# Cosformer attention and a GELU feed-forward on one core: attention recast token-major in full-array matmuls of 65 columns, x transposed by DMA, every load cast to bf16 on Pool's queue

## The chip, the cores and the metric

The kernel runs on one NeuronCore of a Trainium2 chip. A core has a matmul engine (PE, TensorE) with its weight loads (PEld), a vector engine (DVE), a scalar engine (ACT), a general engine (POOL, GpSimd), a sequencer that mostly issues DMAs (SP), and 16 DMA engines. POOL, SP and ACT can each issue DMAs on a queue of their own. Matmul results land in PSUM, eight banks of 512 f32 per partition; everything else is in SBUF. The metric is device time in microseconds (us) of one execution; the median of several runs is compared.

## What is computed

Eight batches of eight heads, 576 tokens, head dimension 64. Each head has linear attention with a cosine and a sine copy of relu(q) and relu(k). The result, as 4608 tokens of 512, goes through two dense layers of 512x2048 and 2048x512 with a sigmoid GELU between them.

```python
B, H, S, D = q.shape                      # 8, 8, 576, 64
theta = np.pi / 2.0 * np.arange(S) / S
cos_w, sin_w = np.cos(theta)[None, None, :, None], np.sin(theta)[None, None, :, None]
def phi(x, c, s):
    r = np.maximum(x, 0.0)
    return np.concatenate([r * c, r * s], axis=-1)
q_p, k_p = phi(q, cos_w, sin_w), phi(k, cos_w, sin_w)
kv  = np.einsum('bhsf,bhsd->bhfd', k_p, v)
z   = np.sum(k_p, axis=2)
num = np.einsum('bhsf,bhfd->bhsd', q_p, kv)
den = np.einsum('bhsf,bhf->bhs', q_p, z)[..., None] + 1e-06
x   = (num / den).transpose(0, 2, 1, 3).reshape(B * S, H * D)
h   = x @ w_in
out = (h / (1.0 + np.exp(-1.702 * h))) @ w_out
```

## The kernel before, in words

**Feed-forward.** The 4608 tokens are cut into nine blocks of 512. `xT` holds x transposed, 512 features in four groups of 128 partitions, all tokens along the row. In block `i`, `mm1(i, fc)` makes one of 16 slices of h: four matmuls of 512 columns (L373) into a PSUM tile `mm`, then a GELU on ACT into bf16 `g` (L378). `mm2` makes the output of 128 tokens at a time: 16 matmuls of 512 columns (L409), a copy to `ysb` on ACT (L419), and a store from POOL's queue (L421). The loop over `n` from 0 to 31 (L542) writes out a block's order by hand: `n` below 16 are the `mm1`, the others groups of four `mm2` matmuls. Block 0 goes through its four output tiles side by side, so that each quarter of `w_out` is needed in turn.

**Attention of the next batch.** Between those groups of block `i`, for `i` from 0 to 6, stand pieces of the attention of batch `b = i + 1`, put at chosen `n` by `at(n, ...)` (L511 to L541). Batch 0 is done ahead of block 0 (L444 to L504). Every engine runs its instructions in the order written. A batch has 576 tokens and a block 512, so the feed-forward falls behind attention by 64 tokens a block, and blocks 7 and 8 have no attention beside them.

**Steps of a batch.** A chunk `c` is 128 tokens (the last, the tail, 64). Tokens of the first 512 are dealt four to a partition, so that a partition's load is 1 KB in a row.

- Loads (`load_part`, `load_tail`, L76 to L103): q, v and k in f32, on SP's queue, each a main part and a tail. Batch 0's tails go on ACT's queue.
- `prep_q` (L216): relu of q to bf16 `qn`, no weights yet.
- Transpose of q: on PE for batches 0 and 1 (`transpose_pe`, L231), by five DMA transposes on SP's queue for the rest (`transpose_dma`, L243). After it DVE multiplies by cosine and sine of each token (`trig`, L241 and L253), giving `qT`, head pairs on partitions, tokens along the row.
- `prep_v` (L262): v times cosine and v times sine, two copies, into `vt`, with two more columns of cosine and sine for the denominator. `prep_k` (L255): relu of k into `kr`.
- `unit_kv` (L277): 40 matmuls of 130 columns, two heads side by side in halves of the array (L285).
- `unit_den` (L306): 32 matmuls of 144 columns in quarters of the array give denominators with tokens along the row (L315); DVE inverts them and splits each number into two bf16 parts.
- `unit_spread` (L359), for each half of the tokens: eight matmuls (L333) repeat the inverses over the 64 rows of each head; ACT copies them to SBUF (L352).
- `unit_num` (L364), for each half: 16 matmuls of 288 columns in quarters of the array (L346), then DVE multiplies by the inverses, straight into `xT` (L357). No transpose of x is needed.

PSUM is split into four `mm` and four `at` tiles of one bank each.

**Order of the loads.** Batch 0's loads stand at the head of SP's queue. The weights are cast from f32 to bf16 by DMAs on POOL's queue. Small instructions that touch a loaded tile keep them in order: POOL's copy of one element of v (L463) holds back `w_in`, a DMA of two bytes of `w_in` on SP (L466) holds back batch 1's loads, POOL's copy from batch 1's k (L479) holds back `w_out`, and one more DMA on SP (L481) holds back batch 2's loads. From batch 3 on, `load_all` runs at `n` = 1 of a block, behind the DMA transposes on SP's queue.

`warmup(n)` (L69) issues matmuls on zeros before and between the steps of batch 0.

Of the kernel before, what the change touches and what calls it, by code (L numbers as in the profile page):

```python
# [2 lines left out]

# [16 lines left out]
GE = mybir.AluOpType.is_ge  # L20
LE = mybir.AluOpType.is_le
ADD = mybir.AluOpType.add
SUB = mybir.AluOpType.subtract
AND = mybir.AluOpType.bitwise_and
# [4 lines left out]
def kernel(  # L29
# [13 lines left out]
    NP = H // 2  # L43
    FC = d_ff // 128
    TB = 512
    NBLK = B * S // TB
    HF = S // 2
    NSEG = 4
    SEG = S // NSEG
    VW = 2 * D + 2  # L50
# [3 lines left out]
    two = ctx.enter_context(tc.tile_pool(name="two", bufs=2))  # L54
    ps = ctx.enter_context(tc.tile_pool(name="ps", bufs=1, space=PSUM))
    ctx.enter_context(tc.manual_schedule())

# [6 lines left out]
    def at_tile():  # L66
        return ps.tile([128, TB], F32, name="at", bufs=4)
# [5 lines left out]

    state = {b: {} for b in range(B)}

    def load_part(t, src, b, h0, h1):  # L76
        nc.sync.dma_start(  # L77
            out=t[:, 256 * h0:256 * h1].rearrange("p (h e) -> p h e", h=h1 - h0),
            in_=src[b, h0:h1, 0:512, :].rearrange("h (p c) d -> p h (c d)", c=4))

    def load_tail(t, src, b, on):
        on.dma_start(
            out=t[0:64, 2048:2560].rearrange("p (h d) -> p h d", h=H),
            in_=src[b, :, 512:576, :].rearrange("h p d -> p h d"))

    SRC = (("qf", q), ("vf", v), ("kf", k))

    def load_new(b):
        for name, _ in SRC:
            state[b][name] = two.tile([128, 2560], F32, name=name)  # L90

    def load_tails(b, on):
        for name, src in SRC:
            load_tail(state[b][name], src, b, on)

    def load_mains(b):
        for name, src in SRC:
            load_part(state[b][name], src, b, 0, H)

    def load_all(b):  # L100
        load_new(b)
        load_mains(b)
        load_tails(b, nc.sync)  # L103

    load_new(0)
    s0 = state[0]
    load_part(s0["qf"], q, 0, 0, 8)
    load_part(s0["vf"], v, 0, 0, 8)
    load_part(s0["kf"], k, 0, 0, 4)
    load_part(s0["kf"], k, 0, 4, 8)  # L110
    load_tails(0, nc.scalar)


    tmp = ExitStack()
    tpool = tmp.enter_context(tc.tile_pool(name="tmp", bufs=1))
# [3 lines left out]
    pos_i = const.tile([128, 5], I32)  # L119
    nc.gpsimd.iota(pos_i[:, 0:4], pattern=[[1, 4]], base=0, channel_multiplier=4)  # L120
    nc.gpsimd.iota(pos_i[:, 4:5], pattern=[[1, 1]], base=512, channel_multiplier=1)
    sel_i = tpool.tile([128, NSEG, 2], I32)
    for j in range(NP):

        nc.gpsimd.iota(sel_i[32 * j:32 * j + 32], pattern=[[-4, NSEG], [16 if j % 2 else -16, 2]],
                       base=-16 * (j % 2), channel_multiplier=1)
    col_i = tpool.tile([128, S], I32)
    nc.gpsimd.iota(col_i[:, 0:512], pattern=[[1, 4], [4, 128]], base=0, channel_multiplier=0)
    nc.gpsimd.iota(col_i[:, 512:576], pattern=[[1, 64]], base=512, channel_multiplier=0)
    id_i = tpool.tile([128, 128], I32)  # L130
    nc.gpsimd.iota(id_i, pattern=[[1, 128]], base=0, channel_multiplier=-1)
    row_i = const.tile([128, 1], I32)
    nc.gpsimd.iota(row_i, pattern=[[0, 1]], base=0, channel_multiplier=1)
    pos_f = const.tile([128, 5], F32)
    nc.vector.tensor_copy(pos_f, pos_i)
    col_f = tpool.tile([128, S], F32)
    nc.vector.tensor_copy(col_f, col_i)
    ident = const.tile([128, 128], BF16)
    nc.vector.tensor_scalar(ident, id_i, 0.0, None, op0=EQ)
    sinw = const.tile([128, 5], F32)  # L140
    cosw = const.tile([128, 5], F32)
    nc.scalar.activation(sinw, pos_f, AF.Sin, scale=scale)
    nc.scalar.activation(cosw, pos_f, AF.Sin, scale=-scale, bias=halfpi)
    trig = const.tile([128, 2, S], BF16)
    nc.scalar.activation(trig[:, 0, :], col_f, AF.Sin, scale=-scale, bias=halfpi)
    nc.scalar.activation(trig[:, 1, :], col_f, AF.Sin, scale=scale)
# [3 lines left out]
    sel_f = tpool.tile([128, NSEG, 2], F32)  # L150
    sel_a = tpool.tile([128, NSEG, 2], F32)
    sel = const.tile([128, NSEG, 2, 64], BF16)
    nc.vector.tensor_scalar(sel_f, sel_i, 2.0, None, op0=LE)
    nc.vector.scalar_tensor_tensor(sel_a, sel_i, 0.0, sel_f, op0=GE, op1=MUL)
    nc.vector.tensor_copy(sel, sel_a.unsqueeze(3).to_broadcast([128, NSEG, 2, 64]))
    tmp.close()

    gpool = ctx.enter_context(tc.tile_pool(name="gpool", bufs=18))
    ypool = ctx.enter_context(tc.tile_pool(name="ypool", bufs=4))

    kr = one.tile([128, 5, NP, 128], BF16, name="kr")
    vt = one.tile([128, 5, H, VW], BF16, name="vt")
    nc.gpsimd.memset(kr[64:128, 4], 0.0)
    nc.gpsimd.memset(vt[64:128, 4], 0.0)
    for c in range(5):
        np_ = 128 if c < 4 else 64
        for cs, w in enumerate((cosw, sinw)):
            nc.gpsimd.tensor_copy(
                vt[:np_, c, :, 128 + cs:129 + cs],
                w[:np_, c:c + 1].unsqueeze(1).to_broadcast([np_, H, 1]))  # L170

    e0 = float(np.float32(1e-6).astype(ml_dtypes.bfloat16))
    e1 = float(np.float32(1e-6 - e0).astype(ml_dtypes.bfloat16))
    e2 = float(np.float32(1e-6 - e0 - e1).astype(ml_dtypes.bfloat16))
    ones = const.tile([3, 128], BF16)
    epsm = const.tile([3, SEG], BF16)
    by_row = const.tile([128, 8], F32)
    bits = const.tile([128, 2], I32)  # L180
    nc.gpsimd.memset(ones, 1.0)
    nc.vector.tensor_scalar(row_i, row_i, 3, None, op0=AND)
    for n, (r, x) in enumerate(((0, -65535.0), (1, -255.0), (1, -65536.0), (2, -256.0), (0, e0), (1, e1), (2, e2))):
        nc.gpsimd.tensor_scalar(by_row[:, n:n + 1], row_i, float(r), x, op0=EQ, op1=MUL)
    nc.gpsimd.tensor_scalar(by_row[:, 0:1], by_row[:, 0:1], by_row[:, 1:2], -1.0, op0=ADD, op1=ADD)
    nc.gpsimd.tensor_tensor(by_row[:, 1:2], by_row[:, 2:3], by_row[:, 3:4], op=ADD)
    nc.gpsimd.tensor_copy(bits, by_row[:, 0:2])
    nc.gpsimd.tensor_tensor(by_row[:, 7:8], by_row[:, 4:5], by_row[:, 5:6], op=ADD)
    nc.gpsimd.tensor_tensor(by_row[:, 7:8], by_row[:, 7:8], by_row[:, 6:7], op=ADD)
    nc.gpsimd.tensor_copy(epsm, by_row[0:3, 7:8].to_broadcast([3, SEG]))  # L190

    zbuf = [one.tile([128, NP, 2, 48], BF16, name=f"zbuf{i}") for i in range(2)]
    for t in zbuf:
        nc.gpsimd.memset(t, 0.0)

    w_in_sb = one.tile([128, NP, d_ff], BF16)
    w_out_sb = one.tile([128, FC, d_model], BF16)
    win_r = moe_w_in.rearrange("(kc p) f -> p kc f", p=128)  # L200
    wout_r = moe_w_out.rearrange("(fc p) d -> p fc d", p=128)
    xT = one.tile([128, NP, B * S], BF16)


    def prep_new(b):
        s = state[b]
# [9 lines left out]
    def prep_q(b, par, on=nc.vector):  # L216
# [11 lines left out]
        if par == 0:  # L228
            relu(on, o[0:64, 4], it)
# [360 lines left out]
```

## Time and profile before

| | us |
|---|---|
| median of 5 runs | 315.0 (314.68 to 316.48) |
| the profiled execution: time | 316.48 |
| its span | 314.7 |
| ACT busy | 136.1 |
| L373 and L409, 512-column matmuls, busy | 128.3 and 125.7 |
| out stores, POOL's issues (L421), busy | 29.5 |

The span is what the profile covers; the run's time lies a little over it. PE's busy time counts a matmul from its start to its end, and ends overlap the next start, so that 512-column matmuls have a mean of 380 ns while they start 216 ns apart. PEld is the loading of weights, which overlaps matmuls. DMA share is the mean busy share of the 16 DMA engines; packets under way together can bring it over 1. Rows such as `L285 PE MATMUL at<-vt,kr 128*64 128x130` read: line 285, result tile from moving and weight tile, the part of the array in use (rows x columns), partitions x columns of the moving tile. In brackets at the end of a timeline's row stands how long the engine had been idle and what ended it.

### The profile page before, as it was taken

The page shows a single profiled execution, that of the slowest core. Times are in us where ns is not written, and L with a number is a line of the kernel's source. Part 1 is how long each engine was busy: PE and PEld are TensorE (multiplying, and loading weights), DVE is VectorE, ACT ScalarE, POOL GpSimd, SP SyncE. Part 2 cuts the span into 40 slices and gives each one's busy share as a digit, 9 for nine tenths or more (in the row PEclk, how much of TensorE's full clock was granted, in tenths as well). Part 3 has the DMA queues.
Part 4 walks back from the last instruction along what each step waited for, and adds up shares of the span by engine and source line. Part 5 has one row for each costly group of instructions (what it writes and reads, how often), then busy time and mean ns, then how long its engine had stood idle before and what let it go on. Part 6 is the DMA issues. An engine that isn't in the chain of part 4 may idle for free.

```text
span 314.7 us, 5588 instructions
## 1 busy us (share of the span) xinstructions
PE 298.8 (95%) x2170; PEld 140.6 (45%) x2208; DVE 134.8 (43%) x341; ACT 136.1 (43%) x263; POOL 47.3 (15%) x106
## 2 busy tenths in 40 slices
PE   8779959999999999999999999999999999999994
PEld 3443434445444544454445444544454444444443
DVE  4860782296339523952295229531953110000000
ACT  5545411355335533553355434543463346226511
POOL 7800060100121011000210120001200220011021
PEclk9998979999999999999999999999999999999998
DMA  7999979996945692489157924791510320011022
GB/s 218 274 203 261 206 116 200 340 240 163 319 98 115 187 284 80 112 245 244 45 116 222 260 65 118 226 251 70 108 36 0 69 67 0 35 67 34 2 67 67
DMA packets 60126, 45.85 MB, mean 146 GB/s; under 512 B 28932, under 2 KB 57860, under 8 KB 60100
## 3 DMA queue, kind: packets, MB, share of 16 engines
q1 hardware_dynamic: 51028, 31.60, 39.2%
q0 software_dynamic: 7328, 13.37, 19.0%
q10 hardware_dynamic: 1744, 0.52, 0.8%
q8 instruction: 17, 0.28, 0.4%
q14 instruction: 9, 0.07, 0.1%
HBM read 36.70 MB, written 9.44 MB: 147 GB/s over the span
## 4 chain that ended last, share of the span: by engine, by line
PE 83%; issue 8%; DMA 5%; POOL 1%; ACT 0%; DVE 0%; SPq 0%; DVEq 0%; ACTq 0%; POOLq 0%
PE mm L409 39%; PE mm L373 35%; DMA vf<-in_v_dram 3%; PE at L346 3%; PE at L285 2%; DMA w_out_sb<-in_moe_w_out_dram 2%; PE at L315 1%; POOL w_in_sb L465 1%; PE mm L433 1%; PE at L333 1%; ACT g L378 0%; DVE xT L357 0%; SPq L77 0%; DVE ysb L438 0%; POOL junk L479 0%
## 5 line engine op out<-in xcount | busy, mean ns | idle before, releaser
L373 PE MATMUL mm<-xT,w_in_sb 128*128 128x512 bf16 x559 | 128.3, 382 | 2.0 <-DVE xT L357 1.2
L409 PE MATMUL mm<-w_out_sb,g 128*128 128x512 bf16 x539 | 125.7, 380 | 1.4 <-DMA w_out_sb<-in_moe_w_out_dram 0.3
L378 ACT ACTIVATE g<-mm 128x512 bf16<-128x512 f32 x144 | 85.5, 598 | 55.6 <-PE mm L373 53.3
L373 PEld LDWEIGHTS <-w_in_sb 128*128 128x128 bf16 x576 | 55.9, 98 | 68.9 <-issue 3.9
L409 PEld LDWEIGHTS <-g 128*128 128x128 bf16 x560 | 52.0, 98 | 63.9 <-issue 3.2
L421 POOL DMA_DIRECT2D out_dram<-ysb x54 | 29.5, 549 | 234.7 <-ACT invb L352 126.1
L419 ACT COPY ysb<-mm 128x512 f32<-128x512 f32 x34 | 19.9, 590 | 87.4 <-PE mm L409 57.6
L357 DVE TENSOR_TENSOR xT<-at,invb 128x288 bf16<-128x288 f32 x60 | 23.3, 450 | 65.2 <-PE at L346 65.2
L352 ACT COPY invb<-at 128x288 f32<-128x288 f32 x60 | 19.7, 421 | 20.4 <-PE at L333 20.4
L438 DVE COPY ysb<-mm 128x256 f32<-128x256 f32 x1 | 0.4, 424 | 56.7 <-PE mm L433 56.7
L253 DVE TENSOR_TENSOR qT<-qTr,trig 128x1152 bf16<-128x1152 bf16 x24 | 16.6, 753 | 17.4 <-DMA qTr<-qn 14.4
L274 DVE TENSOR_SCALAR vt<-vf,cosw 128x512 bf16<-128x512 f32 (+1 forms) x40 | 18.9, 481 | 2.1 <-DMA vf<-in_v_dram 2.1
L214 DVE TENSOR_SCALAR qn<-qf 128x512 bf16<-128x512 f32 (+2 forms) x52 | 14.4, 340 | 9.8 <-DMA qf<-in_q_dram 9.8
L274 DVE TENSOR_SCALAR vt<-vf,sinw 128x512 bf16<-128x512 f32 (+1 forms) x36 | 17.2, 479 | 0.0
L285 PE MATMUL at<-vt,kr 128*64 128x130 bf16 x320 | 11.7, 233 | 4.7 <-DVE kr L214 2.9
L285 PEld LDWEIGHTS <-kr 128*64 128x64 bf16 x320 | 10.2, 116 | 8.2 <-DVE kr L214 3.4
L214 DVE TENSOR_SCALAR kr<-kf 128x1024 bf16<-128x1024 f32 (+1 forms) x23 | 12.7, 601 | 0.0
L72 PE MATMUL mm<-warm 128*128 128x512 bf16 x39 | 11.1, 446 | 1.2 <-DVE halfpi L118 1.2
L346 PE MATMUL at<-qT,kvs 64*64 64x288 bf16 x240 | 10.6, 289 | 0.2 <-DVE den L321 0.2
L346 PEld LDWEIGHTS <-kvs 64*64 64x64 bf16 x256 | 6.2, 106 | 6.7 <-issue 6.4
L323 DVE TENSOR_SCALAR den<-at 128x144 f32<-128x144 f32 x7 | 2.2, 307 | 13.4 <-PE at L315 13.3
L324 DVE RECIPROCAL den<-den 128x144 f32<-128x144 f32 x7 | 7.4, 1053 | 0.2
(72 smaller groups left out, 97.2 us busy)
## 6 DMA issues: line engine op xcount, KB each, us to landing
qf<-in_q_dram SPq DMA_DIRECT2D x8, 1024.0 KB, 5.9
vf<-in_v_dram SPq DMA_DIRECT2D x8, 1024.0 KB, 9.3
kf<-in_k_dram SPq DMA_DIRECT2D x6, 1024.0 KB, 12.3
out_dram<-ysb POOLq DMA_DIRECT2D x38, 128.0 KB, 2.5
out_dram<-ysb POOLq DMA_DIRECT2D x16, 256.0 KB, 2.6
kf<-in_k_dram SPq DMA_DIRECT2D x4, 512.0 KB, 9.8
w_in_sb<-in_moe_w_in_dram POOLq DMA_DIRECT2D x4, 512.0 KB, 9.1
w_out_sb<-in_moe_w_out_dram POOLq DMA_DIRECT2D x4, 512.0 KB, 9.3
```

Of the source, the lines that this page charges most:

```text
L214: on.tensor_scalar(o, i, 0.0, None, op0=MAX)
L253: nc.vector.tensor_tensor(s["qT"][:, j], s["qTr"][:, j].unsqueeze(1).to_broadcast([128, 2, S]), trig, op=MUL)
L274: on.tensor_scalar(o, i, w, None, op0=MUL)
L285: nc.tensor.matmul(kv4[j // 2][w:w + 64, j % 2], kr[:, c, j, 64 * hh:64 * hh + 64], vt[:, c, 2 * j + hh, :], start=(c == 0), stop=(c == 4))
L346: nc.tensor.matmul(tiles[j][w:w + 64, 0:HF], s["kvs"][j][r:r + 64, cs, :], s["qT"][r:r + 64, j, cs, ds(hf * HF, HF)], start=(cs == 0), sto ...
L352: nc.scalar.copy(t, tiles[j][:, 0:HF])
L357: nc.vector.tensor_tensor(xT[:, j, ds(b * S + hf * HF, HF)], tiles[j][:, 0:HF], state[b]["sb", j, hf], op=MUL)
L373: nc.tensor.matmul(hps, w_in_sb[:, kc, ds(fc * 128, 128)], xT[:, kc, ds(i * TB, TB)], start=(kc == 0), stop=(kc == NP - 1))
L378: nc.scalar.activation(g, hps, AF.Gelu_apprx_sigmoid)
L409: nc.tensor.matmul(yps, gT[fc][:, ds(t * 128, 128)], w_out_sb[:, fc, :], start=(fc == 0), stop=(fc == FC - 1))
L419: nc.scalar.copy(ysb, cur[t])
L421: nc.gpsimd.dma_start(out=out[row:row + (n - 1) * step + 1:step, :], in_=ysb[p0:p0 + n, :])
```

## The change

Attention is written anew; the feed-forward, its 512-column matmuls and its stores stay.

- The cosine and sine weights move from q's transposed form and from v to q and k in token-major form. `prep` takes the relu and the weight in one DVE operation: two operations per chunk for q (into `qn`, 128 features a head) and two for k (into `kp`). v is only copied (`prep_v`), with one column of ones beside each head's 64.
- `unit_kv` is 40 matmuls with full 128x128 weights (`kp` of a chunk and head) and 65 columns (v and the ones). The last chunk's lower rows are zeros. Two copies on DVE bring the result to `kvs`.
- `unit_num` works on one chunk: eight matmuls, one a head, with `qT` of the chunk as 128x128 weights and the 65 columns of `kvs`. Tokens are on partitions, so numerator and denominator of a token and head lie in one row; DVE adds 1e-6, inverts eight numbers a token and multiplies 512 columns by them, into `xb`. `unit_den`, `unit_spread` and their tables are gone.
- q's weighted form is transposed by DMA on SP's queue (`turn_q`, five a batch, 1024 columns each), x as well (`turn_x`, five a batch, 512 columns each). Only the first four chunks of batch 0 are transposed on PE, both q and x, with copies by ACT.
- The tail chunk of batch 0 is left for block 0: its `prep` and `turn_q` at `n` = 4, its `unit_num` and `turn_x` at `n` = 9.
- All loads go on POOL's queue and are cast to bf16 on the way, but for batch 0's tails of k and v (f32, SP's queue). Nothing holds them back but buffers and that each POOL DMA waits, in the built program, for the landing of the eighth POOL DMA before it. Order: q, k, v of batch 0, four `w_in`, q of batch 1 and its tail, q's tail of batch 0, one `w_out`, k and v of batch 1 with tails, three `w_out`, all of batch 2. From batch 3 on `load_all` stands at `n` = 1 of the block two before.
- `at` tiles are two of two banks each. The start has 18 and 14 warm-up matmuls; before it had 21, 14 and 4.

```diff
-    HF = S // 2
-    NSEG = 4
-    SEG = S // NSEG
-    VW = 2 * D + 2
+    NC = 5
+    VW = 66
...
     def at_tile():
-        return ps.tile([128, TB], F32, name="at", bufs=4)
+        return ps.tile([128, 2, 512], F32, name="at", bufs=2)
...
+    def load_main(b, n):
+        state[b][n] = t = two.tile([128, 2048], BF16, name=n)
+        nc.gpsimd.dma_start(out=t.rearrange("p (h e) -> p h e", h=H),
+                            in_=SRC[n][b, :, 0:512, :].rearrange("h (p c) d -> p h (c d)", c=4))
+
+    def load_tail(b, n, on=None, dt=BF16):
+        state[b][n, 4] = t = two.tile([64, 512], dt, name=n + "t" + str(dt == F32))
+        (on or nc.gpsimd).dma_start(out=t.rearrange("p (h d) -> p h d", h=H),
+                                    in_=SRC[n][b, :, 512:576, :].rearrange("h p d -> p h d"))
...
+    load_tail(0, "k", nc.sync, F32)
+    load_tail(0, "v", nc.sync, F32)
+    load_main(0, "q")
+    nc.gpsimd.iota(pos_i[:, 0:4], pattern=[[1, 4]], base=0, channel_multiplier=4)
+    nc.gpsimd.iota(pos_i[:, 4:5], pattern=[[1, 1]], base=512, channel_multiplier=1)
+    load_main(0, "k")
+    nc.gpsimd.iota(id_i, pattern=[[1, 128]], base=0, channel_multiplier=-1)
+    load_main(0, "v")
+    for g in range(4):
+        load_w_in(g)
+    load_main(1, "q")
+    load_tail(1, "q")
+    load_tail(0, "q")
+    load_w_out(0)
+    for n in "kv":
+        load_main(1, n)
+        load_tail(1, n)
+    for g in range(1, 4):
+        load_w_out(g)
+    load_all(2)
...
+    def prep(b, n, c):
+        o = state[b]["qn"] if n == "q" else kp
+        for cs, w in enumerate((cosw, sinw)):
+            nc.vector.tensor_scalar(o[:rows(c), c, :, cs * D:cs * D + D], part(b, n, c), 0.0, w[:rows(c), c:c + 1],
+                                    op0=MAX, op1=MUL)
+
+    def prep_v(b, c):
+        nc.vector.tensor_copy(vt[:rows(c), c, :, 0:D], part(b, "v", c))
...
+    def turn_q(b, c):
+        nc.sync.dma_start_transpose(out=q_slot(b, c)[:, :, 0:rows(c)],
+                                    in_=state[b]["qn"][:rows(c), c].rearrange("p h e -> p (h e)"))
+
+    def turn_x(b, c):
+        nc.sync.dma_start_transpose(out=xT[:, :, ds(b * S + c * 128, rows(c))],
+                                    in_=state[b]["xb"][:rows(c), c].rearrange("p h d -> p (h d)"))
...
+    def unit_kv(b):
+        kv = at_tile()
+        for h in range(H):
+            o = kv[:, h // 4, ds(h % 4 * (D + 1), D + 1)]
+            for c in range(NC):
+                nc.tensor.matmul(o, kp[:, c, h, :], vt[:, c, h, 0:D + 1], start=(c == 0), stop=(c == NC - 1))
+        kvs = two.tile([128, 2, 4, VW], BF16, name="kvs")
...
+    def unit_num(b, c):
+        nm = at_tile()
+        for h in range(H):
+            nc.tensor.matmul(nm[:, h // 4, ds(h % 4 * (D + 1), D + 1)], q_slot(b, c)[:, h, :],
+                             state[b]["kvs"][:, h // 4, h % 4, 0:D + 1], start=True, stop=True)
...
+        nc.vector.tensor_scalar(den[:r], nm4[:, :, :, D], 1e-6, None, op0=ADD)
+        nc.vector.reciprocal(inv[:r], den[:r])
+        nc.vector.tensor_tensor(state[b]["xb"][:r, c].rearrange("p (n h) d -> p n h d", n=2), nm4[:, :, :, 0:D],
+                                inv[:r].unsqueeze(3).to_broadcast([r, 2, 4, D]), op=MUL)
...
+    warmup(18)
+    for c2 in range(2):
+        tp = at_tile().bitcast(BF16)
+        for c in (2 * c2, 2 * c2 + 1):
+            prep(0, "q", c)
+            for h in range(H):
+                nc.tensor.transpose(tp[:, c % 2, ts(h, 128)], s0["qn"][:, c, h, :], ident)
+            nc.scalar.copy(qT[:, :, ts(c, 128)], tp[:, c % 2].rearrange("p (h t) -> p h t", h=H))
+    for c in (4, 0, 1, 2, 3):
+        prep(0, "k", c)
+    for c in (4, 0, 1, 2, 3):
+        prep_v(0, c)
+    warmup(14)
+    unit_kv(0)
...
+    unit_num(0, 0)
+    unit_num(0, 1)
+    turn_x_pe(0)
+    unit_num(0, 2)
+    turn_x_pe(1)
+    unit_num(0, 3)
+    turn_x_pe(2)
     first = [mm_tile() for _ in range(4)]
+    mm1_part(first[0], 0, 0, 0, 256)
+    turn_x_pe(3)
+    for fc in (1, 2):
+        mm1_part(first[fc], 0, fc, 0, 256)
+    for fc in range(3):
+        mm1_part(first[fc], 0, fc, 256, 512)
+        gelu(first[fc], fc)
+    mm1_part(first[3], 0, 3)
+    gelu(first[3], 3)
...
+        if i == 0:
+            at(4, prep, 0, "q", 4)
+            at(4, turn_q, 0, 4)
+            at(9, unit_num, 0, 4)
+            at(9, turn_x, 0, 4)
+        elif i + 2 < B:
+            at(1, load_all, i + 2)
         if b < B:
+            k0, k1, k2 = (5, 17, 19) if i == 0 else (0, 12, 17)
             at(k0, prep_new, b)
+            for c in range(NC):
+                at(k0 + c // 2, prep, b, "q", c)
+                at(k0 + c // 2, turn_q, b, c)
+                at(k0 + 5 + c // 2, prep, b, "k", c)
+                at(k0 + 9 + c // 3, prep_v, b, c)
             at(k1, unit_kv, b)
+            for c in range(NC):
+                at(k2 + 2 * c, unit_num, b, c)
+                at(k2 + 2 * c, turn_x, b, c)
```

## Prediction

> **What bounds the kernel now.** I read the page first: which engine is full, and when its clock falls.
>
> ```profile
> PE 298.8 (95%) x2170; PEld 140.6 (45%) x2208; DVE 134.8 (43%) x341; ACT 136.1 (43%) x263; POOL 47.3 (15%) x106
> ...
> PEclk9998979999999999999999999999999999999998
> ```
>
> PE is busy for 95% of the span, and no other engine for half. So what counts is PE's own time in each block, and the stretches early on where PE has nothing to do or a lower clock. Busy time by stretch, cut where PE begins a block's first matmul (PE alone; columns: PE busy, granted clock, DMA share, GB/s), gives the prices:
>
> ```profile
> 15.00:22.00 7.00, 5.52 (x126) 1.00 1.22 203
> 63.34:95.61 32.27, 32.01 (x243) 1.00 0.80 200
> 95.61:127.45 31.84, 31.58 (x245) 1.00 0.66 164
> ...
> 223.11:254.94 31.83, 31.57 (x244) 1.00 0.25 53
> 254.94:282.57 27.63, 27.52 (x128) 1.00 0.10 39
> ```
>
> A block that carries a batch's attention takes 31.84 us, one without it 27.63, which is 128 matmuls of 512 columns, 216 ns from start to start. Attention therefore costs 4.21 us of PE per batch. Blocks 1 to 6, which do batches 2 to 7, run from 63.34 to 254.94, 191.6 us. The start ends at 21.98, and block 0 takes 41.4 us up to 63.34. By 27.63 + 4.21 it would take 31.8, so 9.5 us lie there. The timelines of both, in order of time, show what ends the waits:
>
> ```profile
> 6.89 0.99 DVE L214 TENSOR_SCALAR qn<-qf 128x512 bf16<-128x512 f32 x3 [2.05 <-DMA qf<-in_q_dram]
> ...
> 15.07 1.32 PE L285 MATMUL at<-vt,kr 128*64 128x130 bf16 x40 [1.62 <-ACT kr L212]
> ...
> 21.98 0.81 PE L373 MATMUL mm<-xT,w_in_sb 128*128 128x512 bf16 x3 [0.57 <-DVE xT L357]
> ```
>
> ```profile
> 39.68 0.39 POOL L479 COPY junk<-kf 1x1 f32<-1x1 f32 x1 [24.05 <-DMA kf<-in_k_dram]
> 40.02 4.54 POOL L480 DMA_DIRECT2D w_out_sb<-in_moe_w_out_dram  x4
> ...
> 43.19 2.47 PE L285 MATMUL at<-vt,kr 128*64 128x130 bf16 x40 [2.89 <-DVE kr L214]
> ```
>
> The start is a chain: loads, preparation, 40 matmuls at 15.07, 6.9 us of attention, first matmul. In block 0 PE waits 2.89 us for batch 1's k and goes on at half clock (40 matmuls in 2.47 us instead of 1.32). POOL's touch of `kf` holds the `w_out` loads back until 40.02.
>
> **The change, part by part.** *Attention on PE, blocks 1 to 6.* The 120 matmuls a batch of L285, L315, L333 and L346, which share the array between tiles, go; 40 for `kv` and 40 for the numerators come, each with 128x128 weights and 65 columns. No row has this shape. The price of a matmul with full weights follows from the narrowest views (PE, then PEld):
>
> ```profile
> 34.89 0.22 PE L237 MATMUL at<-ident,qn 128*128 128x128 bf16 x1
> ...
> 34.89 0.39 PE L237 MATMUL at<-ident,qn 128*128 128x128 bf16 x4
> ```
>
> ```profile
> 108.18 0.11 PEld L373 LDWEIGHTS <-w_in_sb 128*128 128x128 bf16 x2
> ```
>
> Three further 128-column matmuls add 0.39 - 0.22 us, 56 ns each, weight loads included. 512 columns take 216 ns. A line through both gives 0.416 ns a column plus 2.7 ns, so 30 ns for 65. Two weight loads of 98 ns fit in 0.11 us, so one can follow another in some 15 ns, which would hide behind 30. The upper end is 56 ns, as if a short stream waited for its weights. I take 32, near the line, and 0.1 us a batch for entries into the sections: 80 x 0.032 + 0.1 = 2.66 us instead of 4.21 (bounds 2.5 and 4.6). Six blocks: 6 x 1.55 = 9.3, and 0.4 that block 1 lost over the others: **9.7 us** (bounds 10.7 and -1.9).
>
> The Trainium skill speaks against this ("TensorE: Matmul & The Clock Gate", sections "LDWEIGHTS" and "Weight-path perf modes"): weights load at 1.2 columns per ns, 107 ns for 128, and the fast mode was measured at about twice that, some 53 ns. By that, an estimate, 80 loads would take 4.3 us a batch and the gain would be nothing. The row with two loads in 0.11 us speaks for the shorter one.
>
> *DVE and ACT.* Per batch DVE loses the four multiplications by `trig`, ten scalings of v, five relus of k, the spread's arithmetic and four products of each half. It gains 20 `prep` operations, five copies and five times (add, reciprocal, product). Their price: 0.48 us by the f32 rows of L274 at 512 elements, 0.33 by the bf16 row of L241 (750 ns for 1152). I take 0.33; the product is priced as the 128x512 copy from PSUM, 0.68 (L417), with 0.17 for each small operation: 1.0 us a chunk. 25 x 0.33 + 5 x 1.0 = 13 us of 30: hidden, at 0.48 too. ACT loses the eight copies of L352.
>
> *Transposes.* Before, five transposes by DMA a batch turn 512 columns of q a token. Now five turn 1024 columns of q and five more 512 of x: three times the work, and PE's transposes of q in block 0 become DMA's too.
>
> ```profile
> qTr<-qn SPq DMA_TRANSPOSE x30, 3.0
> ...
> w_in_sb<-in_moe_w_in_dram POOLq DMA_DIRECT2D x4, 512.0 KB, 9.1
> ```
>
> SP spends 1.27 us on each (median of L248). Twice that for the wide ones: 5 x 2.5 + 5 x 1.27 = 19 us of SP a block, and the last q turn is used 24 us into it. x has 10 us to spare in blocks 1 to 6. Cover exists as long as SP keeps below 30 us a block; beyond that PE waits for SP one to one. SP no longer issues loads, so turns pass none on its own queue, but share the DMA engines with POOL's. In block 0 chunk 3 of x is issued about 5.4 us before block 1 needs it and takes 1.0 + 1.3 + 3.0: 0.5 us of wait.
>
> *Loads.* All on POOL, cast on the way, each waiting for the landing of the eighth before it alone. `w_in` wrote 512 KB in 2.6 us at 203 GB/s. A main part of q, k or v also reads 1 MB and writes 512 KB, but in pieces half as long: 2.6 us if bytes count, 5.2 if pieces do. The plain loads of before moved 341 GB/s between 58.0 and 63.3, 3.1 us for 1 MB, and I take that, nearer to what these loads are. Before, three such and three tails landed from 2.0 to 13.9, so a tail costs 11.9 - 9.3 over 3 = 0.87. Now two tails, three mains and 0.4 for POOL's later start: 2.0 + 1.7 + 9.3 + 0.4 = 13.4 for v, 10.3 for k, 7.2 for q. DVE ends q at 9.8, k at 13.1 (two operations on its tail from 9.8, eight from 10.5), v's four copies at 14.7, and PE starts at 15.0. 40 matmuls: 16.3; `kvs` 16.9; first numerator 17.3; four chunks at 1.0: 18.3 to 21.3; PE turn and ACT copy 1.0: 22.3. Of the first 16 matmuls 1.3 us (twelve of 256 columns on the first two chunks) is done by then: they end at 22.3 + 3.45 - 1.3 = 24.5, where before they end at 21.98 + 0.4 + 3.45 = 25.9. Both lose 1.7 us more to the half clock there. **1.4 us** (bounds: with 0.48 on DVE 0; with 5.2 a main part -4).
>
> In later blocks the six loads stand ahead of the outputs on POOL (L421). An issue of 512 pieces takes 1.0 us (L465) and one of 128 some 0.55 (L421), so 1024 cost about 1.6: 3 x 1.6 + 3 x 1.0 = 8 us from n=1 on, and the first output comes at n=19, 16 us in. Hidden; were it not, `ysb`'s four buffers would hold ACT's copies and then PE's `mm` tiles.
>
> *Block 0.* At 26.2 PE starts n=4, at 31.4 it is past n=9 and wants the turn of q's last 64 tokens of batch 0. That tail stands ninth to tenth in the queue: `w_in` to 23.8, q of batch 1 to 26.9, two tails to 28.7; two `prep` 0.7; the turn 3.0 and 1.3 more for its width: 33.7. **A new wait of 2.3 us** with everything of PE behind it. Then 0.3 and eight groups of 0.86: 40.9 at `unit_kv`. `w_out`'s first part and batch 1's k and v are 3.4 MB, 4.6 with the turns of q beside them: at 3.1 a MB and 0.7 for the last copies ready between 40.0 and 43.7; I take 42.5, 1.6 us of wait (bounds 0 and 2.8). 1.3 for `kv`, 1.7 half clock as before, 14 groups 12.1, five numerators 1.3, 0.5 for x: block 1 starts at **59.4** instead of 63.34.
>
> Sum: 3.9 up to block 1, start included, and 9.7 after it: 13.6 us. The profiled execution has a span of 314.7 and a time of 316.48; the median of five is 315.0, and I take the gain from that: **301 us**.
>
> POOL's issues meet DVE work too. The Trainium skill ("SBUF — State Buffer", "SBUF: two separate sides", the box on the SWDGE trap) says that DVE's fast modes keep POOL from writing descriptors, one long issue instead of a short one. Here L465 took 1.0 us an issue beside DVE work, so I add nothing.
>
> **Rivals.** *Weights show* (56 ns): blocks 1 to 6 gain -1.9 to 0, the start stays: 315 - 3.9 + 1.9 = 313. For it: no row has short streams behind full loads. Against: the two loads in 0.11.
> *DMA becomes the bound* (slower). Share times length gives work per block: 0.66 x 31.8 = 21 with loads, 0.25 x 31.8 = 8.0 without, 0.10 x 27.6 = 2.8 for outputs. So loads 13, turns 5.2. Three times the turns: 13 + 15.6 + 2.8 = 31.4 for a block of 30.3. It decides once turns or loads are late for the next block, above 31.9 of real time. At a tenth more, 34.5: 6 x 2.6 - 3.9 = 12 slower, 327. For it: turns and loads were never under way together before. Against: shares reach 1.22 (15 to 22), so share overstates work.
> *Casting goes by pieces* (5.2 us): three mains 6.3 later, of which DVE's spare time takes 1: start 5 later, block 0 some 3: 309.
> *Block 0 without its waits and half clock*: 2.3 + 1.6 + 1.7 less: 295.4.
>
> **Numbers.** Forecast 0.50, weights 0.12, DMA 0.18, pieces 0.10, no waits 0.10. About 0.5% (1.6 us) is what a measurement can tell from no change. Faster: 0.50 + 0.20 + half of 0.12 = 0.76; same 0.06; slower 0.18. Range 294 to 313: it leaves out DMA and a little at both ends; the forecast's own is 296 to 306.
>
> **What would show it.** Right: blocks 1 to 6 of 30.2 us, starts of the 65-column matmuls 30 to 35 ns apart, a PE wait before the numerator of batch 0's last chunk, DVE under 45%. Wrong: 50 ns and more there; PE waiting on turns in blocks 1 to 6; the first 512-column work after 25; a DMA share near 1.2 throughout.

## The result, and the profile after

The changed kernel takes 316.92 us (median of 38 runs, 315.96 to 319.61) where the kernel before takes 315.69 (75 runs beside them). The ratio is 1.0046, 95% interval 1.0032 to 1.0059: slower by about half a per cent, where 301 us was forecast. The medians here and below are of all runs, while the ratios leave out the few slow ones, among them one of 1070.35 us of the kernel with six turns of q on PE and two buffers. The profiled execution (319.01 us) has a span of 317.2 us, the one of before (316.48 us) 314.7: the spans differ by 2.5 us where the medians differ by 1.2.

The page, its span, busy times and the clock that was granted to TensorE in 40 slices:

```profile
span 317.2 us, 4917 instructions
...
PE 289.3 (91%) x1867; PEld 144.7 (46%) x1900; DVE 103.6 (33%) x347; ACT 115.9 (37%) x193; POOL 97.3 (31%) x115
...
PEclk9897999669997999999999999999999999999999
```

PE is 9.5 us less busy than before (298.8), yet the span grew: PE's share fell from 95% to 91%, and the clock shows a new hole in slices 8 and 9 (56 to 71 us). Cut by blocks (columns: PE busy and instructions, granted clock, DMA share, GB/s), the loss has a place:

```profile
24.98:73.44 48.46, 35.29 (x230) 0.87 1.14 155
73.44:107.33 33.89, 31.73 (x205) 0.95 1.23 156
107.33:137.43 30.10, 29.89 (x205) 1.00 1.13 154
227.73:257.83 30.10, 29.89 (x205) 1.00 0.47 94
257.83:285.46 27.63, 27.53 (x127) 1.00 0.11 39
```

Block 0 took 41.36 us before and takes 48.46; block 1 took 32.27 and takes 33.89; the later blocks with a batch took 31.6 to 32.3 and take 30.1. The start is 3.0 us later (24.98 against 21.98). So up to block 1's first matmul 10.1 us are lost (73.44 against 63.34), blocks 1 to 6 give 7.2 back (184.4 against 191.6), the end 0.4: 2.5 us, the difference of the spans.

What PE waits for in block 0 is in the timeline of the changed kernel (start, length, engine, line, operation; in brackets the idle time before it and what ended it):

```profile
28.19 0.54 DVE L163 TENSOR_SCALAR qn<-qtFalse,cosw 64x512 bf16<-64x512 bf16 x1 [2.63 <-DMA qtFalse<-in_q_dram]
29.02 1.30 SPq L174 DMA_TRANSPOSE qT_tail<-qn  x1
36.13 0.43 PE L200 MATMUL at<-kvs,qT_tail 128*128 128x65 bf16 x8 [0.87 <-DMA qT_tail<-qn]
36.21 0.35 DVE L163 TENSOR_SCALAR qn<-q,cosw 128x512 bf16<-128x512 bf16 x1 [7.22 <-DMA qT_tail<-qn]
36.93 16.80 SPq L174 DMA_TRANSPOSE qT<-qn  x5
53.82 18.68 SPq L178 DMA_TRANSPOSE xT<-xb  x6
62.48 0.69 DVE L208 TENSOR_TENSOR xb<-at,inv 128x512 bf16<-128x512 f32 x1 [13.76 <-DMA xT<-xb]
63.32 0.59 PE L200 MATMUL at<-kvs,qT 128*128 128x65 bf16 x8 [9.33 <-DVE den L206]
```

Read it downwards as one chain. The turn of q's tail is issued at 29.02 and lands 7.1 us later. `qn` has one buffer, so DVE cannot write batch 1's q before that: 7.22 us idle. SP then needs 16.8 us to issue five turns of q. Behind them, at 53.82, stands the turn of x for batch 0's tail, though its product was ready at 40.4. `xb` has one buffer as well, so DVE's product for batch 1's first chunk waits 13.76 us for that turn, and PE, which needs the `at` buffers emptied, waits 9.33. The clock is halved for 10.24 us (58.21 to 68.45). About half of that passes while PE still waits; PE works through the other 5.1 us at half speed, some 2.6 us of loss.

### The profile page after: what moved, and what is told of

Same layout as the page of the kernel before. It is cut to its first block, busy times and chain, and to the rows that moved or that the text cites. A ratio compares the mean times of both kernels' runs of the same rounds, so it can differ in the third digit from the quotient of the medians.

```text
span 317.2 us, 4917 instructions
## 1 busy us (share of the span) xinstructions
PE 289.3 (91%) x1867; PEld 144.7 (46%) x1900; DVE 103.6 (33%) x347; ACT 115.9 (37%) x193; POOL 97.3 (31%) x115
## 4 chain that ended last, share of the span: by engine, by line
PE 74%; DMA 17%; SPq 4%; ACT 1%; issue 1%; DVE 1%; POOL 0%; ACTq 0%; POOLq 0%; DVEq 0%
PE mm L251 34%; PE mm L216 34%; DMA qtFalse<-in_q_dram 5%; DMA qT<-qn 4%; SPq L174 4%; PE at L200 3%; DMA k<-in_k_dram 3%; DMA xT<-xb 3%; DMA qT_tail<-qn 2%; PE at L187 2%; ACT g L221 1%; PE mm L275 1%; POOL q L76 0%; DVE qn L163 0%; DVE xb L208 0%
## 5 line engine op out<-in xcount | busy, mean ns | idle before, releaser
L216 PE MATMUL mm<-xT,w_in_sb 128*128 128x512 bf16 (+1 forms) x571 | 127.3, 377 | 0.9
L263 POOL DMA_DIRECT2D out_dram<-ysb x54 | 49.9, 929 | 195.9 <-ACT ysb L261 195.4
L208 DVE TENSOR_TENSOR xb<-at,inv 128x512 bf16<-128x512 f32 (+1 forms) x40 | 27.6, 689 | 15.3 <-DMA xT<-xb 13.8
L200 PE MATMUL at<-kvs,qT 128*128 128x65 bf16 x312 | 17.0, 198 | 14.8 <-DVE den L206 9.3
L200 PEld LDWEIGHTS <-qT 128*128 128x128 bf16 x312 | 15.2, 101 | 24.6 <-issue 11.1
L280 DVE COPY ysb<-mm 128x256 f32<-128x256 f32 x1 | 0.4, 423 | 59.4 <-PE mm L275 59.4
L163 DVE TENSOR_SCALAR qn<-q,cosw 128x512 bf16<-128x512 bf16 x32 | 11.1, 347 | 11.8 <-DMA qT_tail<-qn 7.2
L187 PEld LDWEIGHTS <-kp 128*128 128x128 bf16 x320 | 11.0, 97 | 2.4 <-issue 0.2
L187 PE MATMUL at<-vt,kp 128*128 128x65 bf16 x320 | 11.6, 193 | 0.0
L163 DVE TENSOR_SCALAR kp<-k,sinw 128x512 bf16<-128x512 bf16 x32 | 11.5, 358 | 0.0
L163 DVE TENSOR_SCALAR qn<-q,sinw 128x512 bf16<-128x512 bf16 x32 | 11.4, 356 | 0.0
## 6 DMA issues: line engine op xcount, KB each, us to landing
w_in_sb<-in_moe_w_in_dram POOLq DMA_DIRECT2D x4, 512.0 KB, 14.4
```

The source lines that it names most:

```text
L163: nc.vector.tensor_scalar(o[:rows(c), c, :, cs * D:cs * D + D], part(b, n, c), 0.0, w[:rows(c), c:c + 1], op0=MAX, op1=MUL)
L187: nc.tensor.matmul(o, kp[:, c, h, :], vt[:, c, h, 0:D + 1], start=(c == 0), stop=(c == NC - 1))
L200: nc.tensor.matmul(nm[:, h // 4, ds(h % 4 * (D + 1), D + 1)], q_slot(b, c)[:, h, :], state[b]["kvs"][:, h // 4, h % 4, 0:D + 1], start=Tru ...
L208: nc.vector.tensor_tensor(state[b]["xb"][:r, c].rearrange("p (n h) d -> p n h d", n=2), nm4[:, :, :, 0:D], inv[:r].unsqueeze(3).to_broadca ...
L216: nc.tensor.matmul(hps[:, c0:c1], w_in_sb[:, kc, ds(fc * 128, 128)], xT[:, kc, ds(i * TB + c0, c1 - c0)], start=(kc == 0), stop=(kc == KC ...
L263: nc.gpsimd.dma_start(out=out[row:row + (n - 1) * step + 1:step, :], in_=ysb[p0:p0 + n, :])
```

## Experiments

Each is an edit of the changed kernel; times are device medians, and "ratio" is to the kernel before, run beside it.

**The two suspects in block 0: the single buffer, and loads beside turns.** First a second buffer for `xb`:

```diff
-        state[b]["xb"] = one.tile([128, NC, H, D], BF16, name="xb")
+        state[b]["xb"] = two.tile([128, NC, H, D], BF16, name="xb")
```

> One edit: xb gets two buffers, so that batch 1's first product need not wait until batch 0's tail is transposed out of xb. Theory A (the single xb buffer, with the transpose of x standing behind five transposes of q on SP, makes the 9.5 us wait of PE in block 0 and the half clock after it): the wait at 53.6 falls below 3 us, block 0 ends 8 us or more earlier, span 317.2 to 305-309. Rival B (the transposes are slow because POOL's loads share the DMA engines; x would then be late for block 1 itself): the wait moves to the first matmul of block 1 or to later numerators and stays above 6 us in sum, span 312 or more.

Measured: 309.68 us, ratio 0.9795 (0.9741 to 0.985), span 308.3. Second, batch 2's loads held back on POOL until batch 0's last turn of x has landed:

```diff
-    load_all(2)
...
+    def load_gated(b):
+        nc.gpsimd.tensor_copy(junk[:, 0:1], xT[0:1, 0, 512:513])
+        load_all(b)
...
+            at(10, load_gated, 2)
```

> One edit: batch 2's six loads are held back on POOL until the transpose of x of batch 0's tail has landed; xb keeps one buffer. Rival B (contention of loads and transposes): the five q transposes of batch 1, which took 16.8 us of SP, take 8 or less, that transpose lands before 49 instead of 62.5, the wait shrinks from 9.5 to under 2 us and the span to 306-309. Theory A alone (order and single buffer, transposes about as slow without the loads): the transpose lands after 57, the wait stays above 5 us, span 312 or more.

Measured: 310.42 us, 0.9825 (0.9779 to 0.9871), span 309.0. The five turns still take 13.14 us of SP, not 8 or less. PE's wait through the single `xb` shrinks to 1.40 us, and one of 5.61 us for x stands at block 1's first matmul:

```profile
53.34 0.41 PE L199 MATMUL at<-kvs,qT 128*128 128x65 bf16 x8 [1.40 <-DVE den L205]
...
66.78 13.44 PE L215 MATMUL mm<-xT,w_in_sb 128*128 128x512 bf16 x51 [5.61 <-DMA xT<-xb]
```

And both together:

> Both edits: two xb buffers and batch 2's loads held back. If either cause alone is enough for the wait, this gives what the better of the two singles gives, within 1 us. If both add (A and B), the span is 2 us or more below both singles: 303-305.

Measured: 308.49 us, 0.9767 (0.9721 to 0.9812), span 306.1. With two buffers alone the 9.33 us wait is gone, but smaller ones come in its place. PE in block 0 of that kernel:

```profile
49.42 0.43 PE L200 MATMUL at<-kvs,qT 128*128 128x65 bf16 x8 [0.72 <-DMA qT<-qn]
53.62 0.43 PE L200 MATMUL at<-kvs,qT 128*128 128x65 bf16 x8 [2.04 <-DMA qT<-qn]
57.43 0.43 PE L200 MATMUL at<-kvs,qT 128*128 128x65 bf16 x8 [1.66 <-DMA qT<-qn]
60.84 0.43 PE L200 MATMUL at<-kvs,qT 128*128 128x65 bf16 x8 [1.25 <-DMA qT<-qn]
```

PE now waits for a turn of q at four of the five chunks: five turns still take SP 17.4 us. With the loads held back too, the turns are quicker and the wait moves to x, which now meets those loads:

```profile
36.59 13.22 SPq L173 DMA_TRANSPOSE qT<-qn  x5
49.90 8.94 SPq L177 DMA_TRANSPOSE xT<-xb  x6
64.55 12.95 PE L215 MATMUL mm<-xT,w_in_sb 128*128 128x512 bf16 x52 [5.15 <-DMA xT<-xb]
```

So neither suspect is the whole cause. Either one removed gives 2% of the changed kernel's time, both give only a little more.

**Warm-ups at the start.**

```diff
-    warmup(14)
+    warmup(2)
```

> One edit: the second train of warm-up matmuls is 2 long instead of 14. Theory C (the start lost its time because PE was still running warm-up matmuls, at half clock, when k and v were ready at 14.9): the kv matmuls start before 15.8 instead of 18.7 and the first 512-column matmul some 2 to 3 us earlier than 29.7; the span gains only what the later waits of block 0 leave, 0 to 3 us. Rival D (the train keeps the clock up, without it the attention of batch 0 runs at half clock longer): kv starts before 15.8 too, but the first 512-column matmul comes less than 1 us earlier or later than before.

Measured: 317.04 us, 1.0041 (1.001 to 1.0073), span 314.8. Block 0 starts at 21.39, 3.6 us earlier, and lasts 51.50 instead of 48.46: PE waits 4.70 instead of 0.87 us for the turn of q's tail. At this point of the study the start was worth nothing, because block 0 has a wait of its own.

**Loads later still.** Two buffers, and batch 2's loads held back until batch 1's chunk 3 of x has landed (the same touch at `xT[0:1, 0, 960:961]`, placed at n=26):

> Two xb buffers, and batch 2's loads held back until chunk 3 of batch 1's x has been transposed. In the run before, held back only until batch 0's tail was, PE waited 5.3 us for x at the first matmul of block 1. If that wait is contention with those loads: below 1.5 us, half clock after it gone, block 1 starts before 61 (64.55), span 301-304. Rival (the late loads of batch 2 then make q of batch 2 late): a wait of 2 us or more before the first numerator of block 1, span 305 or more.

Measured: 310.25 us, 0.9845 (0.9782 to 0.9907), span 308.0. Block 0 falls to 34.17 us and block 1 starts at 59.40, but block 1 takes 38.59: its k and v are late. PE in block 1:

```profile
73.42 0.59 PE L186 MATMUL at<-vt,kp 128*128 128x65 bf16 x3 [2.63 <-DVE vt L166]
...
76.48 2.14 PE L186 MATMUL at<-vt,kp 128*128 128x65 bf16 x36 [1.90 <-DVE vt L166]
```

Holding loads back moves the wait from one block into the next. But block 0 itself is short here although its six turns of q are still on SP.

**Where the chain begins.** If the place of q's tail in the load order starts the chain, loading it first (in float32, on SP) should help:

```diff
+    load_tail(0, "q", nc.sync, F32)
...
-    load_tail(0, "q")
```

Alone, with nothing else changed:

> The changed kernel with one edit: q's tail of batch 0 loaded at the head of SP's queue in f32. In the changed kernel that tail landed at 28.2, its transpose at 36.1, and only then could DVE write q of batch 1 into qn and SP begin its five transposes at 36.9. If the place of this load starts the chain: the five begin before 31, x of the tail is transposed 5 us or more earlier than 62.5, the 9.5 us wait shrinks to under 5, span 308-312. Rival (the transposes crawl as long as POOL's loads run, whenever they start): x of the tail still comes after 59 and the span stays within 2 us of 317.

Measured: 315.98 us, 0.9998 (0.9963 to 1.0032), span 314.2. The turn of the tail is issued at 27.60, only 1.4 us earlier, since DVE does that `prep` in its order behind the numerators of the start, and it needs as long to land as before (7.1 us). The wait of the end is still there, only 1.4 us shorter:

```profile
27.60 1.29 SPq L174 DMA_TRANSPOSE qT_tail<-qn  x1
...
62.95 0.59 PE L200 MATMUL at<-kvs,qT 128*128 128x65 bf16 x8 [7.89 <-DVE den L206]
```

With the two buffers, the later loads and 2 warm-ups beside it:

> As the last, and q's tail of batch 0 loaded at the head of SP's queue in f32 instead of tenth on POOL's, with the second warm-up train cut from 14 to 2. Theory: the shorter train gave 3.6 us at the start and lost them at the numerator of batch 0's tail, which waited 4.9 us for that load and its transpose; with the load early the gain stays: first block's matmuls before 22, no wait over 1 us before that numerator, span 3 us or more below the run without these two edits. Rival: block 0 is then set by the landing of batch 1's k and v, a wait of 3 us or more at batch 1's kv, and the span gains less than 1.5.

Measured: 311.73 us, 0.989 (0.9814 to 0.9965), span 310.8. PE no longer waits for the turn of q's tail, but 3.49 us for a later turn of q (at 51.34) and 1.26 us at batch 1's `kv`. And with a second buffer for `qn` on top (`one.tile` to `two.tile` in its line):

> As the last, with two buffers for qn, so that preparing q of batch 1 does not wait for the transpose of batch 0's tail out of qn. If that buffer still sets when q of batch 1 is transposed: its first transpose 2 us or more earlier and the span 1 us or more lower. Otherwise the same within 1 us.

Measured: 312.98 us, 0.9916 (0.9882 to 0.9949), span 310.3. Batch 1's turns are issued from 28.20 on instead of 36.93, and take SP 19.47 us instead of 16.80: issued earlier, they crawl longer. Neither beats the simpler kernels.

**Is it the cast?** Two buffers, and batch 1's main parts loaded as float32:

```diff
+        if b == 1:
+            state[b][n] = t = one.tile([128, 2048], F32, name=n + "f")
+        else:
+            state[b][n] = t = two.tile([128, 2048], BF16, name=n)
```

> Edit: the kernel with two xb buffers, and batch 1's main parts of q, k and v loaded as float32 without a cast (still on POOL's queue, in the same order). If the cast is what makes the early loads long, the 3072 pieces of batch 1 take some 46 to 55 ns each instead of 59 to 64: about 1.5 to 2 us of the sixteen queues less before 45 us, the last turn of batch 1's q lands that much earlier, and the span falls from 308.3 to about 306.5. If the crawl comes from transposes and loads being under way together, whatever their kind, the five turns still take about 17 us of SP and the span stays within 1 us of 308.3. The preparation of batch 1 costs DVE 0.48 instead of 0.34 an operation; DVE is not what block 0 waits for, so nothing for that.

Measured: 311.96 us, 0.9892 (0.9856 to 0.9929), span 309.3; the five turns take 16.81 us. No gain (with the cast it was 309.68): the early stretch is no shorter. The edit doesn't isolate the cast, though: each of these loads now writes 1024 KB instead of 512, and DVE takes 0.48 us instead of 0.34 for a `prep` of them; PE waits 0.59 us for v at batch 1's `kv`. The same with batch 2 held back:

> Edit: two xb buffers, batch 2's loads held back until batch 0's last turn of x has landed, and batch 1's main parts loaded as float32 without a cast. Beside the same kernel with the cast (span 306.1, five turns in 13.2 us): if the cast is the cost, 1.5 to 2 us less; if not, the same within 1 us.

Measured: 312.75 us, 0.9905 (0.9871 to 0.9939), span 311.7, 5.6 above its partner with the cast. Neither expectation held; PE waits 5.52 us for the turn of q's tail (at 39.43) where the partner waits 0.94.

**A third of the loads moved back.** Two buffers; batch 2's q loads early, only its k and v wait:

> Edit: two xb buffers, and of batch 2 only k and v held back until batch 0's last turn of x has landed; q of batch 2 loads early. If early DMA work is one sum that must be done before about 90 us, moving a third of it back only moves the wait: five turns between 13.2 and 17.4 us of SP, block 0 between 39.7 and 44.5 us, block 1 between 30.1 and 31.7, span 306 to 308.5. If instead what counts is only that x of batch 1 meets no loads, block 0 is near 38 and block 1 at 30.1: span about 303.5.

Measured: 314.05 us, 0.9958 (0.9927 to 0.9988), span 312.2, worse than both expectations. The held loads are issued from 55.84 on, while SP issues the turns of x (53.24 to 63.2), and PE waits 8.98 us for x at 70.73. With all of batch 2 held back the loads met the turns of x as well (issued from 52.74 on), and the wait was 5.15. So a load costs time where it meets a turn that PE is about to need; why it costs more here isn't shown.

**The turns themselves.** What all the kernels so far share are six turns of q on SP in block 0. Here PE does them, 8 transposes a chunk into an `at` tile, and ACT copies them out:

```diff
+    def turn_q_pe(b, cs):
+        tq = at_tile().bitcast(BF16)
+        for c in cs:
+            r = rows(c)
+            for h in range(H):
+                nc.tensor.transpose(tq[:, c % 2, ds(h * 128, r)], state[b]["qn"][:r, c, h, :], ident[:r, :r])
+            nc.scalar.copy(q_slot(b, c)[:, :, 0:r], tq[:, c % 2].rearrange("p (h t) -> p h t", h=H)[:, :, 0:r])
...
-            at(4, turn_q, 0, 4)
+            at(7, turn_q_pe, 0, (4,))
...
-                at(k0 + c // 2, turn_q, b, c)
+                if i > 0:
+                    at(k0 + c // 2, turn_q, b, c)
+                elif c % 2 == 0:
+                    at(11 + c, turn_q_pe, b, range(c, min(c + 2, NC)))
```

With two `xb` buffers:

> Edit: two xb buffers, and in block 0 alone the six turns of q (batch 0's last 64 tokens and batch 1's five chunks) done by PE and copied out by ACT, so that SP's queue holds only turns of x until block 1. If block 0 is long because turns by DMA and loads are under way together and the turns stand one behind another on SP, then without these six batch 1's numerators wait for nothing, x turns as soon as it is there, and block 0 takes 27.6 of matmuls, 2.7 of attention, 1.7 of half clock and 2.5 for 48 transposes on PE, some 35 to 37 us from the same start of about 24: block 1 starts near 60 instead of 68.3, and the span is about 300 instead of 308.3. If the loads alone set it, and batch 1's k and v or x come as late as before, block 1 starts within 2 us of 68.3 and the span stays at 308; PE's and ACT's extra work would show as no loss then.

Measured: 305.74 us (four runs: 304.10, 305.13, 306.36 and 1070.35), 0.9671 (0.9568 to 0.9773), span 303.4. Block 0 takes 37.00 us (expected 35 to 37), and PE waits in it for nothing but ACT's copies, 1.16 us twice:

```profile
25.33 1.06 PE L224 MATMUL mm<-xT,w_in_sb 128*128 128x256 bf16 x4
...
39.49 0.61 PE L182 MATMUL at<-ident,qn 128*128 128x128 bf16 x8 [1.16 <-ACT qT L183]
...
43.43 0.61 PE L182 MATMUL at<-ident,qn 128*128 128x128 bf16 x8 [1.16 <-ACT qT L183]
...
62.33 11.39 PE L224 MATMUL mm<-xT,w_in_sb 128*128 128x512 bf16 x52
```

Then with the single buffer, as the change has it:

> Edit: the changed kernel with its single xb buffer, and in block 0 alone the six turns of q done by PE and copied out by ACT. If the single buffer by itself costs the 9.5 us that PE waited in block 0, a wait of that kind stays: batch 1's product on chunk 0 of x still waits for the turn of batch 0's tail, and the span is 4 us or more above the 303.4 of the same kernel with two buffers. If the buffer hurts only because that turn stands behind five slow turns of q on SP, the turn is issued at about 38.3, lands before batch 1's product at about 49, and the span is 303.4 within 1 us.

Measured: 305.04 us, 0.965 (0.9608 to 0.9692), span 301.8. SP and DVE in block 0 of this kernel:

```profile
35.17 0.68 DVE L216 TENSOR_TENSOR xb<-at,inv 64x512 bf16<-64x512 f32 x1
35.89 23.52 SPq L186 DMA_TRANSPOSE xT<-xb  x6
49.62 0.69 DVE L216 TENSOR_TENSOR xb<-at,inv 128x512 bf16<-128x512 f32 x1
```

The tail's product ends at 35.85, its turn is issued at 35.89 because nothing stands before it on SP, and the next product, 13.7 us later, has no bracket: it waits for nothing. The single buffer costs nothing once the queue ahead of that turn is empty. (Block 0 takes 37.01 us here and 37.00 with two buffers; the spans differ because this execution starts block 0 at 23.34 and the other at 25.33, with the same instructions up to there.) Last, two buffers, q on PE and 2 warm-ups:

> Edit: two xb buffers, the six turns of q of block 0 on PE, and 2 instead of 14 warm-up matmuls ahead of batch 0's kv. In the changed kernel alone fewer warm-ups let block 0 start 3.6 us earlier and the time did not move, since PE then waited longer for the turn of q's tail. With that turn on PE the wait is gone: if PE's order at the start is the cost, block 0 starts at about 22 instead of 25.3 and the span is 300 to 301.5; if the loads (the tail of q lands at 28.3) still decide, block 0 is as much longer as it starts earlier, and the span stays at 303.

Measured: 302.02 us, 0.9555 (0.9514 to 0.9597), span 300.4, as the first of the two expectations has it for the span; block 0 starts at 22.83, a little later than its 22. Its six runs (301.04 to 303.21) lie below all six with 14 warm-ups beside them (303.62 to 305.41; one buffer). The same edit was worth nothing while PE waited for the turn of q's tail. This is the fastest version of the study, 4.5% below the kernel before.

## Why the prediction was wrong

**The price of attention on PE held.** 40 matmuls for `kv` and a group of numerators in a steady block, with DVE's three operations behind the group:

```profile
118.56 1.37 PE L187 MATMUL at<-vt,kp 128*128 128x65 bf16 x40
124.08 0.42 PE L200 MATMUL at<-kvs,qT 128*128 128x65 bf16 x8
124.53 0.17 DVE L206 TENSOR_SCALAR den<-at 128x8 f32<-128x8 f32 x1 [3.81 <-PE at L200]
124.73 0.20 DVE L207 RECIPROCAL inv<-den 128x8 f32<-128x8 f32 x1
125.01 0.69 DVE L208 TENSOR_TENSOR xb<-at,inv 128x512 bf16<-128x512 f32 x1
```

One matmul takes 0.19 us from start to end, so the 40 start (1.37 - 0.19) / 39 = 30 ns apart: the line through 128 and 512 columns gave 30. A batch costs PE 30.10 - 27.63 = 2.47 us (predicted 2.66), and a steady block 30.10 (predicted 30.2). The estimate that spoke against it, some 53 ns a weight load (the Trainium skill, "TensorE: Matmul & The Clock Gate", sections "LDWEIGHTS" and "Weight-path perf modes"), would have made the batch 4.3 us; the measurement decides. That loads can follow one another in 15 ns, as the prediction read from two of them, isn't shown: these rows show only that 30 is enough. The rival "weights show" falls. DVE's prices held too: 0.34 to 0.36 from start to end for a `prep` (0.33; in a row they start 0.27 apart), 0.69 for the product (0.68), 0.17 and 0.20 for the small ones (0.17). DVE is at 33%.

**"9.7 us" for blocks 1 to 6** came out as 7.2. The steady blocks agree; block 1 lost 3.8 against them, 1.95 of it a wait for a turn of q that ends at 98.25 and most of the rest half clock after it (3.41 us, from 99.17 on). The step took block 1 for a steady one.

**"PE starts at 15.0" failed, not the loads.** DVE's copies of v end at 14.87 (predicted 14.7), so "casting goes by pieces" (5.2 us a main part) did not happen at the start either. That the two times agree is partly luck: q came at 8.5 instead of 7.2 and k about 1 us late, and DVE made it up by starting a `prep` every 0.27 us instead of 0.33. What failed is that PE's own order before `kv` was left out. PE at the start:

```profile
10.94 1.05 PE L294 MATMUL at<-ident,qn 128*128 128x128 bf16 x16 [1.10 <-ACT qT L295]
13.56 0.79 PE L294 MATMUL at<-ident,qn 128*128 128x128 bf16 x8 [1.57 <-ACT qT L295]
14.14 4.73 PE L68 MATMUL mm<-warm 128*128 128x512 bf16 x14
18.70 1.37 PE L187 MATMUL at<-vt,kp 128*128 128x65 bf16 x40
```

The transposes of q are paced by ACT's copies of 1.01 us, and the 14 warm-ups, at half clock until 17.25, stand between them and `kv`, which starts 3.7 us late. With 2 warm-ups `kv` started at 14.72 and block 0 at 21.39. The first 512-column work came at 29.05, which the prediction's own test ("after 25") calls wrong. Where 1.4 us were to be gained, block 0 starts 3.0 us later.

**Block 0 is where it was lost.** The step said "block 1 starts at 59.4 instead of 63.34"; it started at 73.44, 14.0 us late; 4.4 of them are the start's. Three of the step's terms failed. "The turn 3.0 and 1.3 more for its width" took 7.1 us; the wait of 2.3 that was added for it came out as 0.87 only because PE got there late. "Twice that for the wide ones", 2.5 us of SP a turn, is wrong as a rule: at the quickest, width costs SP next to nothing (1.23 against 1.19 us), and beside the loads of block 0 a turn took 16.8 / 5 = 3.4, more than the 2.5. Whether width counts beside loads isn't shown. Turns of 1024 columns in the changed kernel (shortest, median and longest issue in ns; then us to landing), and below them those of 512 columns in the kernel before:

```profile
L174 SPq DMA_TRANSPOSE qT<-qn x35: 1232/1287/5531, 36.9 to 230.7; - x35
...
DMA to landing us min/median/max: 3.2/4.8/14.4
```

```profile
L248 SPq DMA_TRANSPOSE qTr<-qn x30: 1192/1266/2630, 66.8 to 229.2; - x30
...
DMA to landing us min/median/max: 2.3/3.0/4.9
```

And a wait was missing altogether: the product of batch 1's first chunk on the turn of batch 0's tail, through the single `xb`, with five slow turns ahead of that turn on SP. The sum priced each turn by itself and never asked which turn stands last in the queue and what waits for that one. PE's wait for it (9.33 us) and the half clock that followed (some 2.6) make 11.9, more than the 10.1 us by which block 1 starts later than before.

**The term for POOL's issues beside DVE work, put at nothing,** was not nothing, but no wait of PE is traced to it. Beside DVE's `prep` and copies POOL takes 3.72 us (from 11.43 on) to issue the load of q's tail of batch 0, where a load of a tail of q takes 0.72 at the median, and up to 4.83 for an out store, where before the longest was 0.78. The steady blocks take 30.1 all the same.

**The rival "DMA becomes the bound"** named the right clash (turns and loads under way together) in the wrong place. It laid the cost on the steady blocks. There the DMA share of 1.13 times 30.1 is 34 us of work, above the 31.9 from which it was to decide, and PE lost nothing; so the share overstates the work, as the point against this rival said. The clash costs where turns and loads stand just ahead of PE, in blocks 0 and 1.

What is shown: six turns of q on SP, slow beside loads and ahead of the turns of x, make block 0 long. Without them it takes 37.0 us with one buffer or two. It takes both, turns and loads: with two buffers and batch 2's loads held back until block 0 is nearly done, it takes 34.17 with the six turns on SP, and block 1 then pays for the late loads. With the turns off SP and the warm-ups out of the way the time is 302.02, near the 301 of the forecast, but by another kernel than the one it was made for. What stays open is how a turn and a load hold each other up in the DMA engines; no run takes that apart.

## What to carry to other kernels

When work moves onto a queue, write down the queue's whole order in the tightest stretch, and ask for the last entry which buffer waits for it; a single buffer behind a slow queue is a wait even where each entry alone is short. Steady-state prices say little of a start in which all loads are under way: price that stretch from rows taken under the same load. An edit that removes time ahead of another wait shows nothing until that wait is gone, so test it again afterwards.

## What the runs showed of the hardware

- A transpose by DMA costs SP 1.23 us for 1024 columns and 1.19 for 512 at the quickest, but up to 5.5 us, and up to 14.4 us to landing, while loads issued by POOL are under way. The Trainium skill says that DMAs of all issuing engines run on the same 16 DMA engines and interleave ("DMA: Bandwidth & Descriptors", section "Issuing engines are not separate DMA queues"). These runs agree, and add that the issuing engine is held up too.
- Batch 1's loads without the cast, as float32 of twice the bytes written, gave no shorter early stretch than as bf16 (five turns in 16.8 and 17.4 us).
- POOL's issue of a load of 64 tokens of q took 0.72 us at the median, and 3.72 (11.43 to 15.15) beside DVE's `prep` and copies of bf16 tiles (11.54 to 14.87).
- Each hole of half clock between two stretches of full clock in the records is 3.41, 6.83, 10.24 or (once, with q's tail loaded first) 13.65 us long, a multiple of 3.41; a wait of PE of 9.33 us brought 10.24 us of it, half of which passed during the wait.
